# Neighbouring heads as a pair: weights in three pieces of all partitions, values in two transfers a twin, queries and keys in two halves

## The chip, the cores and the metric

The kernel runs on one core of one Trainium2 chip. The metric is the device time of one execution in microseconds; lower is better. The inputs q, k, v and the two weight matrices lie in HBM as 32-bit floats, and the output is written there as 32-bit floats.

## The reference

Cosine attention over 8 batches of 12 heads (448 tokens, 64 elements a head), then a two-layer block with a hard-swish between:

```python
q_n = q / (norm(q, axis=-1) + 1e-06)          # q, k, v: (8, 12, 448, 64)
k_n = k / (norm(k, axis=-1) + 1e-06)
scores = q_n @ k_n.T / tau                    # tau = 0.1
attn = softmax(scores) @ v
x = attn.transpose(0, 2, 1, 3).reshape(3584, 768)
h = x @ w_in                                  # (768, 2048)
out = (h * clip(h + 3, 0, 6) / 6) @ w_out     # (2048, 768)
```

## The kernel before

Two heads of a batch form a *pair*; there are 48 pairs (`HP = 6` a batch), and two successive pairs form a *twin*. The pair number n of a batch holds heads n and n + 6. The index g (0 or 1) names the head within a pair. Tokens are laid out so that partition p of 64 holds seven neighbouring tokens, and the 128 partitions hold the two pairs of a twin: partitions 0 to 63 the first pair, 64 to 127 the second.

`load_qk(j)` (line 189) loads *item* j: the queries or the keys of one twin, 448 KB. Items below 14 are queries where j is even and keys where it is odd, two items a twin. In HBM the stride from head to head is 64 times the stride from partition row to partition row, so two neighbouring heads, one of each pair of the twin, run through 128 partitions evenly, and a second dimension steps from head n to head n + 6. One DMA takes the item. `load_v(d)` (line 201) loads the values of a twin in four DMAs: for each g, and for each half of the partitions, 2 heads x 4 chunks of 64 elements. Half 0 goes to partitions 0 to 63 and half 1 to 64 to 127, with a zeroed chunk for padding.

An item then passes `square` (line 211, on ACT, GpSimd = POOL or VectorE = DVE), `reduce` (228, DVE: sums of squares), `norms` (246, four ACT steps: logarithm, exponential of half of it, logarithm with the epsilon as bias, exponential with minus one, which gives one over the norm plus epsilon), `normalise` (266), a transpose (on TensorE for items below 14, on the DMA crossbar after), and copies into `kz` and `qT` (lines 341 and following). `scores`, `exps`, `values` and `finish_values` do the attention of a pair; `vcast` (285) turns the values into 16-bit operands. The result goes transposed into `xT`, 6 chunks of 128 features, whose rows are in the order of `w_in_sb`.

`w_in_r` (line 88) is the first weight matrix as seen by the loads: features n and n + 6 heads share a chunk, so a chunk of 128 rows is two separate blocks of 64 rows, and a load of `w_in` takes 64 partitions. The list `weights` (line 902) holds eight loads, each issued by one `W` in the plan (`next_weights`, line 908, on the POOL queue, which also casts to 16 bits): four for `w_in` (each 64 partitions x 6 chunks x 1024 columns) and four for `w_out` (128 partitions). `mm1_unit(b, fc)` (line 560) multiplies column chunk fc of `w_in` with the features of batch b; it asserts how many loads must have been issued.

The order on each engine is written out by hand. `PLAN` (line 21) is a list of words for the first 18 pairs, such as `LQ.9` (load item 9), `SQ.6.a.0.7` (square item 6 on ACT), `W`, or `U` (one unit of the second part). From pair 18 on a loop (line 999) runs the same steps pair by pair. During the start TensorE runs matmuls of zeros (`DP` and `D`, lines 914 to 924) between its real work. All loads of queries, keys and values, the crossbar transposes and nearly all stores are issued from the SP queue in the plan's order. Each of these DMAs signals one of eight semaphores in turn, and an issue waits until the DMA that used its semaphore before has landed.

Of the kernel before, what the change touches and what calls it, by code (L numbers as in the profile page):

```python
# [14 lines left out]
EPS = 1e-6  # L15
# [46 lines left out]
def kernel(  # L62
# [22 lines left out]
    assert (S, D, HP, SR) == (448, 64, CC, 64)  # L85


    w_in_r = moe_w_in.tensor.rearrange("(g n p) f -> g p n f", g=2, p=64)
    w_out_r = moe_w_out.tensor.rearrange("(fc p) m -> p fc m", p=128)

    const = ctx.enter_context(tc.tile_pool(name="const", bufs=1))
# [47 lines left out]
    def raw_buffer(j):  # L139
# [3 lines left out]
    nrms = [const.tile([128, 7, 2, D], BF16, name=f"nrm{i}", tag=f"nrm{i}") for i in range(3)]  # L143
    n2s = [const.tile([128, 2, 14], FP32, name=f"n2{i}", tag=f"n2{i}") for i in range(2)]
    rs = [
        [const.tile([128, 2, 14], FP32, name=f"{x}{i}", tag=f"{x}{i}") for x in ("ln", "nr", "le", "r")]
        for i in range(2)
    ]
    bias = const.tile([128, 2], FP32, name="bias", tag="bias")
# [39 lines left out]
    def load_qk(j, *heads):  # L189
        needs(("NM", raw_before(j)))  # L190
        raw_of[j] = raw_buffer(j)
        d = j // 2
        b, n = 2 * d // HP, 2 * d % HP
        f = (q, k)[j % 2 ^ (j >= XJ)][b].rearrange("(g n) (p c) d -> n p g (c d)", g=2, c=7)[n : n + 2]
        f = f.rearrange("n p g x -> (n p) g x")
        g = slice(heads[0], heads[0] + 1) if heads else slice(0, 2)
        nc.sync.dma_start(out=raw_of[j][:, g, :, :].rearrange("p g c d -> p g (c d)"), in_=f[:, g, :])
        whole("LQ", j, heads or (0, 1))
        issued.update(("LQ", j, x) for x in heads or (0, 1))

    def load_v(d):
        needs(("VC", 2 * (d - NV)), ("VC", 2 * (d - NV) + 1))
        b, n = 2 * d // HP, 2 * d % HP
        for g in range(2):
            f = v[b, HP * g + n : HP * g + n + 2].rearrange("i (p c) d -> p i (c d)", c=7)
            t = vr[d % NV][:, 2 * g : 2 * g + 2, :, :].rearrange("p i c d -> p i (c d)")
            for half in range(2):
                o = t[64 * half : 64 * half + 64, :, (1 - half) * D : (5 - half) * D]
                nc.sync.dma_start(out=o, in_=f[:, :, 3 * half * D : (3 * half + 4) * D])

    def square(j, e, c0, n):

# [33 lines left out]
    def norms(d, *items):  # L246
        on_vector, items = "v" in items, tuple(x for x in items if x != "v")

        needs(("NM", 2 * d - 4), ("NM", 2 * d - 3))
        items = items or (0, 1)  # L250
        for x in items:
            needs(("RE", 2 * d + x))
        it = slice(items[0], items[-1] + 1)
        ln, nr, le, r = (t[:, it, :] for t in rs[d % 2])
        nc.scalar.activation(out=ln, in_=n2s[d % 2][:, it, :], func=AF.Ln)
        nc.scalar.activation(out=nr, in_=ln, func=AF.Exp, scale=0.5)
        if on_vector:
            nc.vector.tensor_scalar(out=le, in0=nr, scalar1=EPS, scalar2=None, op0=ALU.add)
            nc.vector.reciprocal(out=r, in_=le)
        else:  # L260
            nc.scalar.activation(out=le, in_=nr, func=AF.Ln, bias=eps_bias)
            nc.scalar.activation(out=r, in_=le, func=AF.Exp, scale=-1.0)  # L262
        for x in items:
            issued.add(("NO", d, x))

    def normalise(j, e, *heads):
        d = j // 2
        needs(("NO", d, j % 2), ("TR", j - 3))
        nrm = nrms[j % 3]
        nrm_of[j] = nrm  # L270
        heads = heads or (0, 1)
        g = slice(heads[0], heads[-1] + 1)
        n = len(heads)
        engines[e].tensor_tensor(  # L274
            out=nrm[:, :, g, :].rearrange("p c g d -> p g c d"),
            in0=raw_of[j][:, g, :, :],
            in1=rs[d % 2][3][:, j % 2, :]
            .rearrange("p (g c) -> p g c", g=2)[:, g, :]
            .to_broadcast([128, n, 7, D]),
            op=ALU.mult,  # L280
        )
        if whole("NM", j, heads):
            raw_of.pop(j)

    def vcast(i, e):
        needs(("LV", i // 2), ("VA", i - NVX, 3))
        t = vr[i // 2 % NV][:, i % 2, 1:5, :]
        f = bass.AP(tensor=t.tensor, offset=t.offset, ap=[t.ap[0], [9 * D, 2], [D, 4], [1, D]])
        o = vx[i % NVX][:, :, 0:D].rearrange("p (g c) d -> p g c d", g=2)
        if e == "v":  # L290
            nc.vector.tensor_reduce(out=o, in_=f.rearrange("p g c (d x) -> p g c d x", x=1), axis=AX.X, op=ALU.max)
            return
        (engines[e].copy if e == "a" else engines[e].tensor_copy)(out=o, in_=f)  # L293
# [266 lines left out]

    def mm1_unit(b, fc):
        needs(*(("CX", i) for i in range(b * HP, (b + 1) * HP)))
        assert len(weights) <= 6 - 2 * (2 * fc // FCN)
        x, g, c0 = xT[b % 2], g_of(b), b % 2 * SR
        ps, key = bank_of(None, 1)
        for cc in range(CC):
            nc.tensor.matmul(  # L567
                ps[:, 0:S],
                w_in_sb[:, cc, fc * 128 : (fc + 1) * 128],
                x[:, cc, 0:S],  # L570
                start=(cc == 0),
                stop=(cc == CC - 1),
            )
        def relu():
            u = sb.tile([128, S], BF16, name="u", tag="u", bufs=3)
            nc.scalar.activation(  # L576
                out=u[:, :], in_=ps[:, 0:S], func=AF.Relu, bias=half_bias, scale=1.0 / 6.0
            )
            post["v"].append(lambda: product(u))

        def product(u):
            nc.vector.scalar_tensor_tensor(  # L582
                out=g[:, fc, c0 : c0 + S],
                in0=u[:, :],
                scalar=1.0,
                in1=ps[:, 0:S],
                op0=ALU.min,
                op1=ALU.mult,
            )
            unread[key] = 0  # L590
            g_done.add((b, fc))

        post["a"].append(relu)
# [299 lines left out]
    for n, x in enumerate("2176"):  # L893
# [4 lines left out]
    units[NP] += [(product_unit, n, x, 2) for n, x in ((9, "7"), (9, "6"), (10, "6"))]  # L898
    units[NP] += [(product_unit, 10, "7", x) for x in range(2)]

    FG = d_ff // 2
    weights = [
        (w_in_sb[64 * g : 64 * g + 64, :, f * FG : (f + 1) * FG], w_in_r[g, :, :, f * FG : (f + 1) * FG])
        for f in range(2)
        for g in range(2)
    ] + [(w_out_sb[:, 4 * f : 4 * f + 4, :], w_out_r[:, 4 * f : 4 * f + 4, :]) for f in range(4)]

    def next_weights():
        o, w = weights.pop(0)
# [54 lines left out]


    for t in vr:
        nc.vector.memset(t[64:128, 0:2, 4, :], 0.0)
        nc.vector.memset(t[0:64, 2:4, 0, :], 0.0)
    zeros = xT[1][:, 0, :]
    nc.vector.memset(zeros, 0.0)  # L970
    nc.vector.memset(eps_bias, EPS)
    nc.vector.memset(half_bias, 0.5)
    make_identity(nc, ident)
    for t in vx:
# [123 lines left out]
```

## Time and profile before

| What | Value |
|---|---|
| Median of 3 runs | 406.0 us (405.98 to 406.21) |
| The profiled execution | 404.91 us |
| Its span | 403.1 us |
| Granted TensorE clock, mean | 1.00 |
| Busy: PE, PEld, DVE, ACT, POOL | 98%, 58%, 71%, 69%, 58% |
| Moved by DMA | 65.32 MB, mean 162 GB/s over the span |
| Loads of values from SP | 96 of 128 KB, median 4.4 us from issue to landing |
| Loads of queries and of keys from SP | 24 and 24 of 448 KB, median 4.4 and 4.9 us |
| Loads of `w_in` and of `w_out` from POOL | 4 and 4 of 768 KB, median 10.2 and 9.2 us |
| Transposes by DMA from SP | 34 into `tT`, 25 into `xT`, median 3.3 and 3.8 us |

PE is TensorE's matmuls, PEld its weight loads, SPq the sync engine's queue. The span runs from the first to the last instruction; the execution's own time is 1.8 us longer than its span, and the median of the runs 1.1 us longer than that execution. All times within the profile count from the start of the span. A size in KB of a weight load is that of the 16-bit data written; twice as much is read. A view of stretches has one row for each: its borders and length, the busy time of each engine with the number of instructions, the granted clock, the busy share of the 16 DMA engines and the GB/s that they moved. A share above 1 is possible, since packets of one engine overlap.

### The profile page before, as it was taken

Reading aid. Unit: us, or ns where it says so; the run is one execution under the profiler, and the core shown is the slowest. Engines: PE = TensorE matmul, PEld = TensorE weight load, DVE = VectorE, ACT = ScalarE, POOL = GpSimd, SP = SyncE. Lnnn points to the kernel's source line nnn. Section 1 sums busy time; section 2 is a strip of 40 time slices with the busy share of each in tenths; the row PEclk is TensorE's granted clock in tenths of the full one; section 3 lists DMA queues with packets and bytes.
Section 4 is the critical chain, followed back from the end, with each engine's and each line's share of the span. In section 5 each row is a group of like instructions: output and inputs, shape, how many; then the busy total and the mean of one; then the engine's idle time right before and its main releaser. Section 6 shows DMA issues by size and latency. Waiting matters only on the chain.

```text
span 403.1 us, 9619 instructions
## 1 busy us (share of the span) xinstructions
PE 395.5 (98%) x3696; PEld 234.3 (58%) x3696; DVE 286.4 (71%) x503; ACT 278.3 (69%) x609; POOL 234.0 (58%) x228
## 2 busy tenths in 40 slices
PE   7999999999999999999999999999999999999996
PEld 4666656555655556556555556555565556555563
DVE  5898768766998777776867888687656566644663
ACT  5999998798467686786858768668658755225230
POOL 7799655662384997488386865766665500510070
PEclk9999999999999999999999999999999999999999
DMA  8999989979988659786989659976963523130134
GB/s 289 281 254 257 216 247 230 156 125 230 187 213 220 139 128 228 171 222 130 180 216 212 152 130 164 182 192 145 192 154 76 112 46 67 41 79 21 26 73 99
DMA packets 91566, 65.32 MB, mean 162 GB/s; under 512 B 56064, under 2 KB 89984, under 8 KB 91520
## 3 DMA queue, kind: packets, MB, share of 16 engines
q1 hardware_dynamic: 87408, 58.02, 62.8%
q0 software_dynamic: 3712, 6.29, 9.0%
q8 instruction: 29, 0.48, 0.5%
q10 hardware_dynamic: 400, 0.39, 0.3%
q14 instruction: 17, 0.14, 0.1%
HBM read 47.19 MB, written 11.01 MB: 144 GB/s over the span
## 4 chain that ended last, share of the span: by engine, by line
PE 94%; DVE 3%; DMA 1%; ACT 0%; issue 0%; DVEq 0%; ACTq 0%
PE M L567 24%; PE M L740 17%; PE PV L462 13%; PE Y L567 6%; PE M L422 6%; PE Z L567 5%; PE Y L740 4%; PE Z L740 4%; PE M L614 3%; PE M L820 2%; PE Z L422 2%; PE PV L922 2%; PE Z L820 1%; PE Y L422 1%; DVE n L238 1%; PE SC L422 1%
## 5 line engine op out<-in xcount | busy, mean ns | idle before, releaser
L440 ACT ACTIVATE at<-M 128x448 bf16<-128x448 f32 x200 | 99.9, 568 | 16.4 <-PE M L422 14.4
L567 PE MATMUL M<-xT,w_in_sb 128*128 128x448 bf16 x522 | 110.8, 352 | 0.0
L567 PEld LDWEIGHTS <-w_in_sb 128*128 128x128 bf16 x768 | 72.0, 98 | 62.6 <-issue 2.8
L274 POOL TENSOR_TENSOR nrm<-big,r 128x896 bf16<-128x896 f32 (+1 forms) x48 | 79.5, 1662 | 26.1 <-ACT r L262 19.3
L576 ACT ACTIVATE u<-M,bias 128x448 bf16<-128x448 f32 x87 | 57.0, 655 | 25.2 <-PE M L567 24.8
L582 DVE SCALAR_TENSOR_TENSOR gT<-u,M 128x448 bf16<-128x448 bf16 x76 | 46.7, 618 | 36.8 <-ACT u L576 36.3
L226 POOL TENSOR_TENSOR big<-big 128x896 f32<-128x896 f32 (+3 forms) x39 | 63.9, 1641 | 10.9 <-DMA big<-in_k_dram 5.7
L462 PEld LDWEIGHTS <-at 128*128 128x128 bf16 (+1 forms) x1536 | 54.9, 97 | 22.8 <-issue 13.5
L462 PE MATMUL PV<-vx,at 128*128 128x65 bf16 (+1 forms) x1536 | 64.3, 194 | 0.2 <-DVE on L483 0.2
L238 DVE TENSOR_REDUCE n<-big 128x14 f32<-128x896 f32 (+1 forms) x50 | 51.7, 1041 | 5.6 <-ACT big L224 4.6
L379 POOL COPY km<-tT 64x128 bf16<-64x128 bf16 x34 | 12.8, 376 | 58.1 <-DMA tT<-nrm 45.1
L769 POOL TENSOR_TENSOR big<-big 128x384 f32<-128x384 f32 x11 | 11.8, 1076 | 54.6 <-ACT big L788 54.5
L740 PEld LDWEIGHTS <-gT 128*128 128x128 bf16 x288 | 27.8, 98 | 20.0 <-DVE gT L718 0.6
L740 PE MATMUL M<-w_out_sb,gT 128*128 128x384 bf16 x208 | 37.9, 326 | 0.1
L440 ACT ACTIVATE at<-Z 128x448 bf16<-128x448 f32 x49 | 27.7, 565 | 9.9 <-PE M L422 7.3
L483 DVE TENSOR_TENSOR on<-PV,rc 128x512 bf16<-128x512 f32 x48 | 33.2, 691 | 1.7
L293 POOL CAST vx<-big 128x512 bf16<-128x512 f32 x44 | 33.2, 757 | 1.2 <-DMA big<-in_v_dram 1.1
L422 PE MATMUL M<-tT,kz 64*128 64x448 bf16 (+1 forms) x175 | 31.6, 351 | 0.0
L740 PEld LDWEIGHTS <-gs 128*128 128x128 bf16 x224 | 21.5, 98 | 14.8 <-DVE gs L718 0.4
L567 PE MATMUL Y<-xT,w_in_sb 128*128 128x448 bf16 x132 | 28.6, 352 | 0.0
L440 ACT ACTIVATE at<-Y 128x448 bf16<-128x448 f32 x45 | 25.7, 570 | 3.1 <-PE Z L422 1.7
L740 PE MATMUL M<-w_sum,gs 128*128 128x384 bf16 x144 | 26.3, 326 | 0.0
(130 smaller groups left out, 561.7 us busy)
## 6 DMA issues: line engine op xcount, KB each, us to landing
big<-in_v_dram SPq DMA_DIRECT2D x96, 128.0 KB, 4.4
big<-in_k_dram SPq DMA_DIRECT2D x24, 448.0 KB, 4.9
big<-in_q_dram SPq DMA_DIRECT2D x24, 448.0 KB, 4.4
out_dram<-o SPq DMA_DIRECT2D x107, 96.0 KB, 2.2
w_in_sb<-in_moe_w_in_dram POOLq DMA_DIRECT2D x4, 768.0 KB, 10.2
w_out_sb<-in_moe_w_out_dram POOLq DMA_DIRECT2D x4, 768.0 KB, 9.2
tT<-nrm SPq DMA_TRANSPOSE x34, 3.3
xT<-on SPq DMA_TRANSPOSE x25, 3.8
```

Source lines behind the costliest of these rows:

```text
L226: engines[e].tensor_tensor(out=o, in0=i, in1=i, op=ALU.mult)
L238: nc.vector.tensor_reduce(out=n2s[d % 2][:, j % 2, c], in_=sq[:, :, :, :].rearrange("p g c d -> p (g c) d")[:, c, :], axis=AX.X, op=ALU.add,)
L274: engines[e].tensor_tensor(out=nrm[:, :, g, :].rearrange("p c g d -> p g c d"), in0=raw_of[j][:, g, :, :], in1=rs[d % 2][3][:, j % 2, :] . ...
L293: (engines[e].copy if e == "a" else engines[e].tensor_copy)(out=o, in_=f)
L422: nc.tensor.matmul(o, ks, qt[rows], start=True, stop=True)
L440: nc.scalar.activation(out=o, in_=x, func=AF.Exp, scale=inv_tau)
L462: nc.tensor.matmul(pv_out(j, h), at[rows, n, q_cols(i // HP, j)], vt[rows, 3 + h if name == "M" else 5 * h + int(name[1]), :], start=(name ...
L483: nc.vector.tensor_tensor(out=on[:, :, :, :].rearrange("p j h d -> p h j d"), in0=pv4[:, :, :, 0:D], in1=rc[:, :, :].to_broadcast([128, 2, ...
L567: nc.tensor.matmul(ps[:, 0:S], w_in_sb[:, cc, fc * 128 : (fc + 1) * 128], x[:, cc, 0:S], start=(cc == 0), stop=(cc == CC - 1),)
L576: nc.scalar.activation(out=u[:, :], in_=ps[:, 0:S], func=AF.Relu, bias=half_bias, scale=1.0 / 6.0)
L582: nc.vector.scalar_tensor_tensor(out=g[:, fc, c0 : c0 + S], in0=u[:, :], scalar=1.0, in1=ps[:, 0:S], op0=ALU.min, op1=ALU.mult,)
L740: nc.tensor.matmul(m, lhs[:, c, :], rhs[:, c, c0 : c0 + width], start=(base is None and c == 0), stop=(c == KC - 1), skip_group_check=True,)
```

## The change

A pair now holds two neighbouring heads, 2n and 2n + 1. The twin's four heads lie next to each other in HBM.

- Queries and keys: from the first pair to the second the stride is now two heads, which doesn't run on evenly from partition 63 to 64. Each item is loaded by two DMAs, one for each half of the partitions, of 64 partitions x 2 heads x 448 elements.
- Values: the four heads of a twin are one dimension, so each half of the partitions is one DMA of 64 x 4 x 256 elements. Two DMAs a twin in place of four. `vcast` and the zeroed chunks follow the new order of heads in the tile.
- `w_in`: a chunk is now 128 neighbouring rows, so a load takes all 128 partitions. Three loads of 512, 512 and 1024 columns stand in place of four, the last `W` of them leaves the plan, and the assertion in `mm1_unit` follows.
- Norms: the tile `nr` is twice as wide, with the epsilon set once in every second place, and `ln` takes the part of `le`. The ACT branch, the only one that the plan uses, keeps its four steps; two memsets are added at the start.

The order of all other instructions on TensorE, ACT, DVE and POOL stays as it was. On SP every load of an item becomes two in a row, and every four loads of values two.

```diff
-    "U RE.13 U SC.8.3 UV UA CQ.10.v VA.7.0 W RE.12 UV CQ.11.a UV UA NO.6 U EX.8.3 VA.7.1 VA.7.2 UV VC.9.p VA.7.3",
+    "U RE.13 U SC.8.3 UV UA CQ.10.v VA.7.0 RE.12 UV CQ.11.a UV UA NO.6 U EX.8.3 VA.7.1 VA.7.2 UV VC.9.p VA.7.3",
...
-    w_in_r = moe_w_in.tensor.rearrange("(g n p) f -> g p n f", g=2, p=64)
+    w_in_r = moe_w_in.tensor.rearrange("(n p) f -> p n f", p=128)
...
-        [const.tile([128, 2, 14], FP32, name=f"{x}{i}", tag=f"{x}{i}") for x in ("ln", "nr", "le", "r")]
+        [const.tile([128, 2, 14, n], FP32, name=f"{x}{i}", tag=f"{x}{i}") for x, n in (("ln", 1), ("nr", 2), ("r", 1))]
...
-        f = (q, k)[j % 2 ^ (j >= XJ)][b].rearrange("(g n) (p c) d -> n p g (c d)", g=2, c=7)[n : n + 2]
-        f = f.rearrange("n p g x -> (n p) g x")
-        g = slice(heads[0], heads[0] + 1) if heads else slice(0, 2)
-        nc.sync.dma_start(out=raw_of[j][:, g, :, :].rearrange("p g c d -> p g (c d)"), in_=f[:, g, :])
+        f = (q, k)[j % 2 ^ (j >= XJ)][b].rearrange("(n g) (p c) d -> n p g (c d)", g=2, c=7)
+        for i in range(2):
+            o = raw_of[j][64 * i : 64 * i + 64, :, :, :].rearrange("p g c d -> p g (c d)")
+            nc.sync.dma_start(out=o, in_=f[n + i])
...
-        for g in range(2):
-            f = v[b, HP * g + n : HP * g + n + 2].rearrange("i (p c) d -> p i (c d)", c=7)
-            t = vr[d % NV][:, 2 * g : 2 * g + 2, :, :].rearrange("p i c d -> p i (c d)")
-            for half in range(2):
-                o = t[64 * half : 64 * half + 64, :, (1 - half) * D : (5 - half) * D]
-                nc.sync.dma_start(out=o, in_=f[:, :, 3 * half * D : (3 * half + 4) * D])
+        f = v[b, 2 * n : 2 * n + 4].rearrange("i (p c) d -> p i (c d)", c=7)
+        t = vr[d % NV][:, :, :, :].rearrange("p i c d -> p i (c d)")
+        for half in range(2):
+            o = t[64 * half : 64 * half + 64, :, (1 - half) * D : (5 - half) * D]
+            nc.sync.dma_start(out=o, in_=f[:, :, 3 * half * D : (3 * half + 4) * D])
...
-        ln, nr, le, r = (t[:, it, :] for t in rs[d % 2])
+        ln, nr, r = (t[:, it, :, 0] for t in rs[d % 2])
...
-            nc.scalar.activation(out=le, in_=nr, func=AF.Ln, bias=eps_bias)
-            nc.scalar.activation(out=r, in_=le, func=AF.Exp, scale=-1.0)
+            nc.scalar.activation(out=ln, in_=nr, func=AF.Ln, bias=eps_bias)
+            nc.scalar.activation(out=r, in_=ln, func=AF.Exp, scale=-1.0)
...
-        t = vr[i // 2 % NV][:, i % 2, 1:5, :]
-        f = bass.AP(tensor=t.tensor, offset=t.offset, ap=[t.ap[0], [9 * D, 2], [D, 4], [1, D]])
+        t = vr[i // 2 % NV][:, 2 * (i % 2), 1:5, :]
+        f = bass.AP(tensor=t.tensor, offset=t.offset, ap=[t.ap[0], [4 * D, 2], [D, 4], [1, D]])
...
-        assert len(weights) <= 6 - 2 * (2 * fc // FCN)
+        assert len(weights) <= 6 - min(2, 4 * fc // FCN)
...
-    FG = d_ff // 2
-    weights = [
-        (w_in_sb[64 * g : 64 * g + 64, :, f * FG : (f + 1) * FG], w_in_r[g, :, :, f * FG : (f + 1) * FG])
-        for f in range(2)
-        for g in range(2)
-    ] + [(w_out_sb[:, 4 * f : 4 * f + 4, :], w_out_r[:, 4 * f : 4 * f + 4, :]) for f in range(4)]
+    pieces = [slice(f * d_ff // 4, f * d_ff // 4 + n * d_ff // 4) for f, n in ((0, 1), (1, 1), (2, 2))]
+    weights = [(w_in_sb[:, :, f], w_in_r[:, :, f]) for f in pieces] + [(w_out_sb[:, 4 * f : 4 * f + 4, :], w_out_r[:, 4 * f : 4 * f + 4, :]) for f in range(4)]
...
+    for t in rs:
+        nc.vector.memset(t[1][:, :, :, 1], EPS)
```

More of the change, by code (lines that the diff above doesn't have):

```diff
@@ L257, in norms @@
         if on_vector:
-            nc.vector.tensor_scalar(out=le, in0=nr, scalar1=EPS, scalar2=None, op0=ALU.add)
-            nc.vector.reciprocal(out=r, in_=le)
-        else:
-            nc.scalar.activation(out=le, in_=nr, func=AF.Ln, bias=eps_bias)
-            nc.scalar.activation(out=r, in_=le, func=AF.Exp, scale=-1.0)
+            nc.vector.tensor_reduce(out=ln, in_=rs[d % 2][1][:, it, :, :], axis=AX.X, op=ALU.add)
+            nc.vector.reciprocal(out=r, in_=ln)
+        else:
+            nc.scalar.activation(out=ln, in_=nr, func=AF.Ln, bias=eps_bias)
+            nc.scalar.activation(out=r, in_=ln, func=AF.Exp, scale=-1.0)
         for x in items:
@@ L276, in normalise @@
             in0=raw_of[j][:, g, :, :],
-            in1=rs[d % 2][3][:, j % 2, :]
+            in1=rs[d % 2][2][:, j % 2, :, 0]
             .rearrange("p (g c) -> p g c", g=2)[:, g, :]
@@ L966 @@
     for t in vr:
-        nc.vector.memset(t[64:128, 0:2, 4, :], 0.0)
-        nc.vector.memset(t[0:64, 2:4, 0, :], 0.0)
+        nc.vector.memset(t[64:128, 0:4:2, 4, :], 0.0)
+        nc.vector.memset(t[0:64, 1:4:2, 0, :], 0.0)
     zeros = xT[1][:, 0, :]
```

## The prediction

> **What bounds the kernel now.** I read the page first: the span, the busy shares and the slices.
>
> ```profile
> span 403.1 us, 9619 instructions
> ...
> PE 395.5 (98%) x3696; PEld 234.3 (58%) x3696; DVE 286.4 (71%) x503; ACT 278.3 (69%) x609; POOL 234.0 (58%) x228
> ...
> PE   7999999999999999999999999999999999999996
> ...
> DMA  8999989979988659786989659976963523130134
> ```
>
> TensorE is the bound: busy 98%, at full granted clock, so nothing that the change does to other engines can buy much. But the DMA slices read 8 to 9 for the first tenth and more of the span, and the stretch in which the attention pipeline fills lives on loads. There the change works. So I next asked for the waits of the start, in order of time.
>
> ```profile
> 3.80 2.71 SPq L209 DMA_DIRECT2D big<-in_v_dram  x4
> ...
> 4.31 0.67 ACT L224 ACTIVATE big<-big 128x192 f32<-128x192 f32 x2 [2.29 <-DMA big<-in_k_dram]
> ...
> 5.51 0.53 ACT L224 ACTIVATE big<-big 128x384 f32<-128x384 f32 x1 [0.54 <-DMA big<-in_q_dram]
> ...
> 7.92 4.04 SPq L209 DMA_DIRECT2D big<-in_v_dram  x4
> ...
> 16.99 1.26 DVE L291 TENSOR_REDUCE vx<-big 128x512 bf16<-128x512 f32 x2
> ```
>
> ACT starts the moment item 1 (keys) lands and again when item 0 (queries) lands. The SP queue runs far ahead of the data, so landings are set by the rate of the DMA engines, not by issuing. That rate is what the third view shows: the same engines in stretches that carry only query/key loads (rows 1, 2, 5) and only value loads (rows 3, 4, 6).
>
> ```profile
> 3.00:5.50 2.50, 2.50 (x14) 1.83 (x13) 1.37 (x9) 0.67 (x2) 1.29 (x6) 1.00 1.06 406
> 5.50:9.50 4.00, 4.00 (x22) 2.24 (x20) 2.18 (x4) 3.05 (x10) 3.18 (x4) 1.00 1.06 381
> 10.00:11.50 1.50, 1.50 (x23) 1.30 (x21) 1.50 (x2) 1.19 (x2) 0.77 (x1) 1.00 1.13 230
> 13.50:15.00 1.50, 1.50 (x15) 1.03 (x13) 1.50 (x4) 1.50 (x3) 1.50 (x2) 1.00 1.14 235
> 16.00:17.50 1.50, 1.50 (x18) 0.78 (x16) 1.50 (x4) 1.41 (x4) 0.98 (x1) 1.00 1.06 382
> 22.50:25.00 2.50, 2.35 (x34) 1.53 (x32) 2.50 (x5) 2.34 (x8) 2.48 (x3) 1.00 1.12 244
> ```
>
> The last column is GB/s. Both kinds keep the engines fully busy (share over 1), yet transfers of 128 partitions move 381 to 406 GB/s and transfers of 64 partitions 230 to 244. The packet records say the same: 1024-byte value packets take 46 ns while a 128-partition transfer is still ahead of them, then 73 to 91 ns among themselves; 1792-byte query/key packets take 74 to 79 ns, but 124 to 126 ns beside value packets. So it is not the packet size; it is that all 16 engines write one half of the partitions at a time.
>
> **Queries and keys in two halves: the price.** Today items land 1.20 us apart (4.29, 5.49, 6.70, 7.90, 9.11): 458,752 bytes at 382 GB/s. Afterwards each is two transfers of 64 partitions, alternating halves as the value loads do now. A value twin of 524,288 bytes takes 2.0 to 2.1 us (10.70 to 12.82, 14.18 to 16.19), 252 GB/s. At that rate an item takes 1.82 us: **0.62 us more per item**. Bounds: 0 if two halves in flight spread over all partitions; 0.80 if every packet takes 126 ns (16 x 126 = 2.0 us). I take 0.62, since value loads have the same shape and the same alternation.
>
> [...]
>
> Issuing: a 64-partition load costs SP 0.60 us (values), a 128-partition one 0.46. Two per item is 0.9 to 1.2 us of issue under 1.82 us of data: hidden. SP also waits for the landing of the eighth DMA before, as in the gaps at 7.92; eight halves in flight are 7 us of data, enough.
>
> **Where it reaches the path.** For each item the landing before, its first reader, the slack, and the shift (0.62 for each item up to it):
> - item 0: 5.49, ACT square 5.51, slack 0.02, shift 1.2: late **1.2**. This goes through reduce, norms and copies to the first scores (12.47).
> - item 2: slack 1.71 (7.90 to 9.61), shift 2.5: 0.8. Item 5: 1.75, shift 3.1: 1.35.
> - item 4: 10.70, POOL square 11.90, slack 1.20, shift 3.7: **2.5**. Its reduce starts on DVE 0.04 us after that square, with the copy of the next keys queued behind.
> - second value twin: 16.19, DVE cast 17.58, slack 1.40, seven items ahead, shift 4.3: **2.9**. Behind it on DVE stands the copy of the next queries (18.18), which releases scores.
> - items 7 and 8: slack 2.48 and 2.92, shift 5.0 and 5.6: 2.5 and 2.7. From 18.5 to 20.5 the engines have some 0.9 us to spare, which comes off from here.
> - item 10: 25.15, POOL square 27.23, slack 2.09, shift 6.5: POOL is 4.4 late. POOL is busy 17.8 of the 18 us from 28 to 46, so it can't catch up, but its results have 0.73 to 1.03 us before TensorE reads them (normalised item 32.90 to 33.63, cast 33.45 to 34.48). That leaves 3.4 to 3.7.
>
> TensorE follows the largest: 2.9 from the values, and up to 0.8 more from item 10. There the rate was already poor (packets of 1792 bytes at 118 to 121 ns beside the weights), so the shift is overstated: half, 0.4. **3.3 us.** After 46 us value casts and squares have 5 us and more of slack until the loop; in the loop, where TensorE is saturated, items are read 0.1 to 10 us after landing by POOL, which has idle time there (58% of the span). One transpose into xT lands 0.04 us before TensorE reads it (126.31 to 126.35), with a key load queued ahead of it on SP: 0 to 0.6; I take 0, as TensorE's 6 matmuls before it give cover when the loads shift together, and keep 0.6 for the range. A lost start is not regained by an engine that is full.
>
> **Weights.** Four loads of 64 partitions become three of 128, 768, 768 and 1536 KB; the issue at 42.89 (0.69 us of POOL) goes and the other three have more descriptors: about nothing. The first matmul that needs them starts at 42.85, 0.3 us after piece two landed; now it needs only piece one. No gain: TensorE wasn't waiting (17.73 of 18.0 us busy). Chunk 8 needs the third piece, at 58.59 + 3.3 = 61.9. Pieces three and four took 13.3 us together (40.00 to 53.33); issued 3.7 late, with three slower items beside it (1.9), it lands near 59. Cover 3 us; if that is gone, see below.
>
> **Values.** 96 transfers become 48 with the same packets to the same halves: no data time, and SP gets back 1.2 us a twin, which pays for the split items. The norms keep four ACT steps (0.21 to 0.32 us); two memsets (0.06 us each) end well before 4.31. Casts read another stride: same 0.61 us. All at nothing; if the stride mattered, 0.1 us of POOL a pair, under its idle time.
>
> **Rivals.**
> - *Not slower.* The halves overlap: engines drift apart, some write low and some high partitions, and an item keeps 1.2 us. It decides at about 0.3 us more per item: below that the second value twin is under 0.8 us late. For it: item halves are larger packets and queued eight deep. Against: the value loads, queued alike, run at 230 to 244 GB/s for microseconds. It gives 406.0, and with the lighter weight writes from 25 to 50 us at best 405.7 (TensorE idles only 0.27 us from 28 to 46). [...]
> - *The third weight piece is late.* Piece two took 13.7 us for half the bytes when loads stood beside it (28.86 to 42.55). At such a pace the big piece lands 3 us or more after chunk 8's turn, and TensorE waits: 409.3 + 3 = 412.3. Against: the SP queue runs dry at 46.55 before the loop's loads.
> - *Slack swallows most.* If only item 0's 1.2 us reaches TensorE, 407.2.
>
> **How the numbers follow.** The profiled execution took 404.9 us; plus 3.3 is 408.2. The median of the runs is 1.1 above the profiled one: 406.0 + 3.3 = 409.3. Chances: forecast 0.56, late piece 0.14, slack 0.14, not slower 0.16, of which 0.12 within 0.2% (0.8 us, about what a measurement of this kernel can tell from no change) and 0.04 faster. Range: 0.80 us per item and 0.6 in the loop give 411.2; the late piece 412.3; slack 407.2; a part of the rival of no change comes in at 406.4. So 406.4 to 412.8; slower 0.84.
>
> **What would show it.** Right: windows that carry only queries and keys at 230 to 260 GB/s; 1792-byte packets near 125 ns; item 0 near 6.7 us, the second value twin near 20.5; first scores near 13.7; first matmul of the weights near 46; from there a constant shift. Wrong: items still 1.2 us apart; DVE's second cast not behind its data; a shift that grows through the loop; TensorE waiting on weights at chunk 8.

## The result, and the profile after

The changed kernel takes 409.11 us (median of 12 runs, 408.45 to 409.94) beside 406.0 us of the kernel before (12 runs, 405.15 to 408.65): the ratio over all runs is 1.0066, with a 95% interval of 1.0048 to 1.0085, which is 2.7 us (1.9 to 3.5) of 406; the medians are 3.1 apart. The forecast was 409.3 us and slower. The profiled execution took 409.91 us against 404.91, which is 5.0 us. That overstates the change: this execution lies 0.8 us above the median of its kernel and that of before 1.1 us below. So the two profiles are used below for places and rates, and the ratios for sizes.

From the page after: the span, the busy shares, and the slices of TensorE and of the DMA engines.

```profile
span 408.0 us, 9617 instructions
...
PE 396.5 (97%) x3696; PEld 234.6 (57%) x3696; DVE 287.2 (70%) x505; ACT 278.7 (68%) x609; POOL 234.3 (57%) x227
...
PE   6798999999999999999999999999999999999996
...
DMA  8999999999999858798599849967974522231033
```

TensorE has the same 3696 matmuls and 1.0 us more of busy time, so the rest of the longer span is waiting. The slices show where: the first two and the fourth are 6, 7 and 8 in place of 7, 9 and 9, while the DMA slices read 9 without a gap from the second to the thirteenth. After that TensorE's strip is as before.

The timeline answers the lines that were shown of before (SP's issues, ACT's first squares, DVE's cast of the values). In brackets stand the idle time ahead and what ended it.

```profile
5.47 0.67 ACT L223 ACTIVATE big<-big 128x192 f32<-128x192 f32 x2 [3.45 <-DMA big<-in_k_dram]
7.41 0.52 ACT L223 ACTIVATE big<-big 128x384 f32<-128x384 f32 x1 [1.27 <-DMA big<-in_q_dram]
...
8.73 1.26 SPq L208 DMA_DIRECT2D big<-in_v_dram  x2
...
21.77 0.69 DVE L290 TENSOR_REDUCE vx<-big 128x512 bf16<-128x512 f32 x1 [0.72 <-DMA big<-in_v_dram]
```

ACT starts on the queries 1.9 us later than before (7.41 against 5.51). The second cast of values, which waited for no load in the kernel before, now does. SP issued the first value load at 8.73 us and its data landed at 16.26, so SP is still far ahead of the data.

The same stretches as before, with the granted clock, the DMA share and the GB/s in the last three columns:

```profile
3.00:5.50 2.50, 2.50 (x14) 1.83 (x13) 0.38 (x8) 0.03 (x1) 0.56 (x5) 1.00 1.06 261
5.50:9.50 4.00, 4.00 (x28) 2.45 (x25) 2.92 (x6) 2.00 (x7) 2.24 (x3) 1.00 1.08 237
10.00:11.50 1.50, 0.67 (x9) 0.51 (x9) 0.00 (x0) 1.44 (x5) 1.50 (x2) 1.00 1.09 232
13.50:15.00 1.50, 1.50 (x9) 0.43 (x6) 1.50 (x5) 1.40 (x5) 0.00 (x0) 0.50 1.10 232
16.00:17.50 1.50, 1.50 (x15) 1.03 (x13) 0.50 (x1) 1.50 (x3) 1.50 (x2) 1.00 1.11 231
22.50:25.00 2.50, 2.50 (x34) 1.47 (x34) 2.13 (x5) 2.04 (x4) 1.50 (x2) 1.00 1.08 234
```

Every stretch of the start now runs at 231 to 261 GB/s, with the engines no less busy than before (share 1.06 to 1.11). The loads of queries and keys have taken on the rate that only value loads had. The halves land 0.97 to 0.98 us apart, so an item takes 1.95 us in place of 1.20, and a packet of 1792 bytes takes 121 to 141 ns in place of 74 to 79.

The chain of work that ended last (start, length, what) says which of the late loads sets the end:

```profile
8.09 7.04 DMA big<-in_q_dram
...
15.14 8.48 DMA big<-in_k_dram
...
23.64 8.67 DMA big<-in_q_dram
...
35.00 1.69 POOL big L225
36.69 1.65 POOL nrm L273
38.39 0.56 PE Z L318 x7
```

Three loads of queries and keys follow each other, each issued when the one eight DMAs before it had landed. The last is the upper half of item 10, landed at 32.31 us. Behind it POOL squares items 10 and 11 and normalises item 7, and for that result TensorE waits with a transpose, at 38.39 us in place of 33.69. An earlier wait of the same kind belongs to item 4, whose upper half landed at 15.13: POOL squares it from 15.29 on, then normalises item 3, which TensorE transposes at 18.67 in place of 15.57. First the rows of the changed kernel, then TensorE's two of the kernel before:

```profile
16.92 1.69 POOL L273 TENSOR_TENSOR nrm<-big,r 128x896 bf16<-128x896 f32 x1
...
18.67 0.56 PE L318 MATMUL Y<-ident,nrm 128*128 128x128 bf16 x7 [0.56 <-POOL nrm L273]
...
38.39 0.56 PE L318 MATMUL Z<-ident,nrm 128*128 128x128 bf16 x7 [1.08 <-POOL nrm L273]
```

```profile
15.57 0.56 PE L319 MATMUL Y<-ident,nrm 128*128 128x128 bf16 x7
...
33.69 0.55 PE L319 MATMUL Z<-ident,nrm 128*128 128x128 bf16 x7
```

Matmul by matmul, TensorE is 1.8 us late at its first scores (14.31), 3.1 at 18.67 and 4.7 at 38.39.

### The profile page after: what moved, and what is told of

The parts are those of the page before. It is cut to its first block, busy times and chain, and to the rows that moved or that the text cites. A ratio compares the mean times of both kernels' runs of the same rounds, so it can differ in the third digit from the quotient of the medians.

```text
span 408.0 us, 9617 instructions
## 1 busy us (share of the span) xinstructions
PE 396.5 (97%) x3696; PEld 234.6 (57%) x3696; DVE 287.2 (70%) x505; ACT 278.7 (68%) x609; POOL 234.3 (57%) x227
## 4 chain that ended last, share of the span: by engine, by line
PE 87%; DMA 7%; SPq 2%; DVE 2%; POOL 1%; issue 1%; POOLq 0%
PE M L566 24%; PE M L739 16%; PE PV L461 11%; PE Y L566 6%; PE M L421 6%; PE Z L566 5%; PE Y L739 4%; DMA big<-in_q_dram 4%; PE Z L739 3%; PE M L613 3%; DMA big<-in_k_dram 2%; PE M L819 2%; SPq L197 2%; PE Z L421 1%; PE Z L819 1%; PE Y L421 1%
```

## Experiments

Each kernel was timed in turns with the kernel before on the same chip. A ratio times 406 gives the distance in us; intervals reach 0.7 to 1.3 us to each side, and the difference of two ratios is good to about 1.2 us.

### Which part costs, which part gains

**The kernel before with each item in two halves of the partitions** (`e1_parts`), and nothing else of the change:

```diff
-        nc.sync.dma_start(out=raw_of[j][:, g, :, :].rearrange("p g c d -> p g (c d)"), in_=f[:, g, :])
+        for i in range(2):
+            r = slice(64 * i, 64 * i + 64)
+            nc.sync.dma_start(out=raw_of[j][r, :, :, :].rearrange("p g c d -> p g (c d)"), in_=f[r, :, :])
```

> The kernel before, with each item of queries and keys loaded by two transfers of 64 partitions each (same bytes, same pairs of heads). If halves of the partitions are the cause: items land about 1.95 us apart in place of 1.20, GB/s in stretches of queries and keys alone near 235, the first scores near 14.3 us in place of 12.5, item 10 lands near 32, and the time is that of the changed kernel, 2.5 to 3.5 us above the kernel before. If weights or values made the loss: within 0.5 us of the kernel before.

Measured: 412.49 us, ratio 1.0155 (1.0124 to 1.0187), 6.3 us, more than twice the whole change. The start is much like that of the changed kernel; its second stretch (5.5 to 9.5 us) reads

```profile
5.50:9.50 4.00, 4.00 (x28) 2.48 (x25) 2.78 (x6) 1.79 (x7) 2.13 (x3) 1.00 1.05 240
```

But here the delay goes on growing: matmul by matmul, this profile is 4.0 us behind that of before at 33.7 us, 5.0 at 126 and 6.2 at 225. Its waits of TensorE (total, times, longest) name the place:

```profile
PE M L568 <- DMA xT<-on: 1.3, 2, 1.0
PE M L423 <- DMA tT<-nrm: 0.6, 1, 0.6
```

These are transposes by DMA, which SP issues behind the loads. With four value loads and four halves a twin, SP has eight loads where both the kernel before and the changed one have six.

**The changed kernel with whole items** (`e3_whole`). The items are again of heads n and n + 6, so queries and keys belong to other pairs than the values:

```diff
-        f = (q, k)[j % 2 ^ (j >= XJ)][b].rearrange("(n g) (p c) d -> n p g (c d)", g=2, c=7)
-        for i in range(2):
-            o = raw_of[j][64 * i : 64 * i + 64, :, :, :].rearrange("p g c d -> p g (c d)")
-            nc.sync.dma_start(out=o, in_=f[n + i])
+        f = (q, k)[j % 2 ^ (j >= XJ)][b].rearrange("(g n) (p c) d -> n p g (c d)", g=2, c=7)[n : n + 2]
+        f = f.rearrange("n p g x -> (n p) g x")
+        nc.sync.dma_start(out=raw_of[j][:, :, :, :].rearrange("p g c d -> p g (c d)"), in_=f[:, :, :])
```

> The changed kernel, with items loaded whole again, 128 partitions in one transfer of heads n and n + 6 (so that queries and keys are of other heads than the values: the output is not the reference's). If halves of the partitions are the cause of all: the time of the kernel before, within 0.8 us, TensorE not idle before the first scores, clock not lowered. If the weights in three pieces or the values in two transfers add to the loss: 0.8 us or more above the kernel before.

Measured: 404.27 us (404.06 to 405.29), ratio 0.9957 (0.994 to 0.9973): 1.7 us faster than before, which neither case of the expectation had. So the halves cost 2.7 + 1.7 = 4.4 us, and the rest of the change gives 1.7 back.

**The two other parts, each alone in the kernel before**: weights in three pieces (`e5_weights`) and values in two transfers a twin (`e6_values`). Each leaves the heads in their old pairs, so rows of the weights, or values, meet other heads than their own; only the time is of use.

```diff
-    w_in_r = moe_w_in.tensor.rearrange("(g n p) f -> g p n f", g=2, p=64)
+    w_in_r = moe_w_in.tensor.rearrange("(n p) f -> p n f", p=128)
...
+    pieces = [slice(f * d_ff // 4, f * d_ff // 4 + n * d_ff // 4) for f, n in ((0, 1), (1, 1), (2, 2))]
```

> The kernel before, with only the input weights changed: three pieces of all 128 partitions (quarter, quarter, half of the columns), one weight load of POOL less; the rows stand in the order of the changed kernel while the heads stay in the old one, so the output matrix is multiplied with rows in another order. Theory 1 (the gain that the whole-item form of the change showed, 1.75 us under the kernel before, comes from SP's shorter queue of value transfers): the weights alone are worth nothing, 405.5 to 406.5 us, and the starts of the matmuls are those of the kernel before until 126 us. [...]

```diff
-        for g in range(2):
-            f = v[b, HP * g + n : HP * g + n + 2].rearrange("i (p c) d -> p i (c d)", c=7)
-            t = vr[d % NV][:, 2 * g : 2 * g + 2, :, :].rearrange("p i c d -> p i (c d)")
-            for half in range(2):
+        f = v[b, 2 * n : 2 * n + 4].rearrange("i (p c) d -> p i (c d)", c=7)
+        t = vr[d % NV][:, :, :, :].rearrange("p i c d -> p i (c d)")
+        for half in range(2):
```

> The kernel before, with only the value loads changed: two transfers of 64 partitions x 4 heads for a twin where there were four of two heads each. The four neighbouring heads that are loaded are not those of the twin's queries and keys, so the output is that of other values. Theory 1 (SP's queue: two issues of about 0.6 us less for each of 24 twins, so that the DMA transposes behind them start earlier): 404.0 to 405.2 us, the matmuls' starts as before until about 126 us and then ever earlier, by 0.7 to 1.5 us. Theory 2 (the weights bring it): 405.7 to 406.5 us.

Measured: weights 406.33 us, ratio 1.0007 (0.9989 to 1.0025), nothing. Values 404.6 us, ratio 0.9982 (0.996 to 1.0004), 0.7 us faster with an interval that just holds no change. That is the side of theory 1, that values bring the gain, but 0.7 is short of the 1.7 of all parts together, and the expected growth of a lead in the loop was not to be read. The profiled execution was a late one (407.48 us), and it had lost its time at the start:

```profile
13.27 0.56 PE L421 MATMUL SC<-tT,kz 64*128 64x448 bf16 x4 [1.64 <-DVE tT L340]
16.09 0.37 PE L421 MATMUL SC<-tT,kz 64*128 64x448 bf16 x2 [1.31 <-ACT at L439]
```

Here item 3 landed at 8.99 us in place of 6.70, though it was issued at the same time and the engines moved 367 GB/s from 5.5 to 9.5 us. So an item that is next in line can come 2.3 us later in one execution than in another of nearly the same loads. The spread of the kernel before (404.7 to 409.4 us on one chip) may be this; no second trace shows it.

### Where in the span the halves cost

**Whole items below 14, halves after** (`e9_late_halves`) and **halves for the first four items alone** (`e11_first_four`), both from the changed kernel. The diff is that of the first; the second has `j >= 4` as its condition:

```diff
+        if j < XJ:
+            f = (q, k)[j % 2][b].rearrange("(g n) (p c) d -> n p g (c d)", g=2, c=7)[n : n + 2]
...
+            nc.sync.dma_start(out=raw_of[j][:, :, :, :].rearrange("p g c d -> p g (c d)"), in_=f[:, :, :])
+        else:
             f = (q, k)[j % 2 ^ (j >= XJ)][b].rearrange("(n g) (p c) d -> n p g (c d)", g=2, c=7)
             for i in range(2):
...
```

> The changed kernel, with the items below 14 whole (heads n and n + 6, as before) and the later ones in two halves of the partitions; the early queries and keys are so of other pairs than the values, and the output is not the reference's. It splits the cost of the halves (409.1 us of the changed kernel less 404.3 us of the one with whole items, 4.8 us) in two. Theory 1 (the cost lies in the start, where items are awaited one after another, as the prediction has it): 404.3 to 405.2 us, the matmuls as in the kernel with whole items until 60 us and at most 0.5 us later at the end. Theory 2 (much of it is the doubled number of transfers in the loop, whose issue delays the transposes behind them on SP): 405.5 to 407.0 us, with the delay growing between 126 and 280 us.

> The changed kernel with only the first four items in halves and all others whole (those of the first 14 that are whole are of heads n and n + 6, so the output is not the reference's). The first four then land as late as in the changed kernel (up to 11.23 us in place of 7.90), and the rest at the old rate. Theory 1 (a lost start is not regained, the prediction's last assumption): the matmuls stay 1.9 to 2.5 us behind the kernel with whole items to the end, 406.1 to 407.2 us. Theory 2 (what counts is the later items that end last, item 10 above all, and the early lateness is swallowed by idle filler matmuls and by buffers): 404.3 to 405.3 us.

Measured: late halves 404.86 us, ratio 0.998 (0.9961 to 0.9999); first four alone 407.12 us, ratio 1.0016 (0.9996 to 1.0035). In us from before: -0.8 and +0.6, beside -1.7 with none and +2.7 with all. So the later halves cost 0.9, the first four 2.4, and, if the three add up, the ten in between the rest of the 4.4, 1.1. The times of both runs lie where theory 1 has them. With halves for four items only, the matmuls are 2.4 us behind those of the kernel with whole items at 13 us and 2.9 to 3.1 from 16 us to the end: a start once lost is not regained, though all later items come whole. It is more than the 2.5 of theory 1, and part of it is not the loads: in that profile TensorE ran at half its clock from 13.2 to 16.6 us, eight of its filler matmuls took 1.66 us in place of 1.02, and it fell 0.6 us further back without a wait. The 0.9 of the later halves is not firm: in its profile the kernel with late halves lies 0.14 us behind the one with whole items at 225 us.

### Why two halves are slow

**Two transfers of all partitions, one for each head of the pair** (`e2_heads`), in the kernel before. Same number of transfers and of bytes as the halves:

```diff
+        for i in range(2):
+            g = slice(i, i + 1)
             nc.sync.dma_start(out=raw_of[j][:, g, :, :].rearrange("p g c d -> p g (c d)"), in_=f[:, g, :])
```

> The kernel before, with each item loaded by two transfers too, but split by head: 128 partitions of 448 elements each. As many transfers, issues and landings as with halves of the partitions. If halves of the partitions are the cause: items stay 1.20 to 1.25 us apart at 370 GB/s or more, and the time stays within 0.8 us of the kernel before. If the number of transfers (two issues of 0.5 to 0.6 us, waits for the eighth landing before) is the cause: items land 1.9 us apart and the time rises by 2.5 to 3.5 us.

Measured: 408.2 us, ratio 1.0048 (1.0029 to 1.0067), 1.9 us, where the halves cost 6.3. The rate from 5.5 us on is that of whole items:

```profile
3.00:5.50 2.50, 2.50 (x14) 1.84 (x13) 1.67 (x9) 0.67 (x2) 1.02 (x6) 1.00 0.85 242
5.50:9.50 4.00, 4.00 (x20) 2.05 (x18) 2.28 (x4) 2.00 (x8) 2.66 (x3) 1.00 1.01 367
```

In the first stretch the engines were partly idle (share 0.85), which put the start 1.0 us late; the loop then added 1.8 (1.0 us behind at 33.7, 2.8 at 272). The 1.9 us lie between the two cases of the expectation: the rate is that of the first, and the number of transfers has a price of its own: with eight loads a twin on SP, the loop loses 1.8 us here and 2.2 in the run by halves. The changed kernel has six again. Its distance to before is 4.7 us at 38.4 us and 5.1 at 131.

Where the data lies in HBM is not the cause either: a transfer by head here and a half of the changed kernel both read two neighbouring heads, 224 KB in one run, and they move 367 and 237 GB/s.

**Every other partition in place of upper and lower halves** (`e12_alternate`), in the kernel before:

```diff
+        for i in range(2):
+            o = raw_of[j][i:128:2, :, :, :].rearrange("p g c d -> p g (c d)")
+            nc.sync.dma_start(out=o, in_=f[i:128:2])
```

> The kernel before, with each item in two transfers of 64 partitions, as in the run by halves, but each transfer takes every other partition of all 128 (even ones, then odd ones) in place of the lower or the upper 64. Nothing is left out. Theory 1 (what halves the rate is where the 64 partitions lie: neighbouring ones share what leads into them): the rate in 5.5 to 9.5 us is over 330 GB/s, the packets of 1792 bytes take about 75 to 90 ns, and the time is that of the two transfers by head, 407.5 to 409 us. Theory 2 (it is the number of partitions or of rows of a transfer, wherever they lie): 230 to 260 GB/s, packets of about 125 ns, 411 to 413.5 us as in the run by halves.

Measured: 456.05 us, ratio 1.122 (1.1187 to 1.1253), far from both theories; but its first 9 us answer the question.

```profile
5.50:9.50 4.00, 4.00 (x26) 2.52 (x24) 2.21 (x5) 1.71 (x7) 1.99 (x3) 1.00 0.97 322
...
13.50:15.00 1.50, 0.00 (x0) 0.00 (x0) 1.50 (x2) 0.39 (x1) 0.00 (x0) 1.00 0.03 11
```

The median packet took 74 ns, as with whole items, and the third, fourth and fifth item each landed 1.2 to 1.7 us after the one before, at 322 GB/s, where halves of the partitions in the same kernel moved 240. Transfers of 64 partitions are thus not slow for having 64 rows: it counts which partitions they are. The rest of the run says nothing on that: from 9 us on engines wait for loads whose data they don't read. In its timeline DVE sums queries and keys only when values have landed, and SP, waiting in turn, lets the DMA engines run dry (share 0.03 in the row above).

```profile
13.49 1.08 DVE L239 TENSOR_REDUCE n<-big 128x14 f32<-128x896 f32 x1 [4.41 <-DMA big<-in_v_dram]
```

**Lower halves on SP's queue, upper halves on ACT's** (`e7_two_queues`), for the first four items of the changed kernel, issued at the very start:

```diff
-            nc.sync.dma_start(out=o, in_=f[n + i])
+            (nc.scalar if i and j < 4 else nc.sync).dma_start(out=o, in_=f[n + i])
```

> The changed kernel, with the loads of its first four items issued at the very start, the lower halves on SP's queue and the upper halves on ACT's (behind its table load, so 1.3 us later than SP's). In the changed kernel upper and lower halves take turns on one queue and move 237 GB/s from 5.5 to 9.5 us. [...] Theory 2 (the cost is in the small rows or in the number of packets, whatever the queue): 225 to 250 GB/s again, the fourth item at 10.8 to 12 us, 408.7 to 409.8 us.

Measured: 408.68 us, ratio 1.0058 (1.0034 to 1.0081), no different from the change. ACT issued its first load at 0.76 us, beside its table load (0.74 to 2.02 us) and not behind it, so upper and lower halves were in flight together from 3 to 10 us. The rate rose only a little:

```profile
5.50:9.50 4.00, 4.00 (x19) 1.95 (x17) 2.40 (x6) 1.88 (x7) 1.75 (x3) 1.00 1.07 265
```

265 GB/s in place of 237 is a little above the 225 to 250 of theory 2, and the fourth item landed at 10.69 us in place of 11.23, a little ahead of its 10.8 to 12. Having both halves in flight doesn't restore 380 GB/s: a packet took about 119 ns whether few or most of the packets beside it were of the other queue. Two queues moved 12% more than one queue on which the halves take turns.

### The clock, and two other versions

**More filler matmuls at the start of the changed kernel** (`e8_filler`), so that TensorE doesn't run idle ahead of its first transposes:

```diff
-RE.0.0 DP.8 NO.0.0 ... TR.1.Y DP.2 TR.0.Z
+RE.0.0 DP.18 NO.0.0 ... TR.1.Y DP.10 TR.0.Z
```

> The changed kernel with 18 more filler matmuls, 10 ahead of the first transposes and 8 ahead of the second, so that TensorE does not run idle at 9.5 to 10.8 and 11.6 to 12.6 us. In the profile of the changed kernel its granted clock is 0.5 from 12.3 to 15.7 us. Theory 1 (the clock is halved since TensorE ran idle, and the stretch at half clock costs nothing, since item 10's landing at 32.3 us sets the start): the granted clock is 1.0 throughout, and the time stays, 408.7 to 409.5 us. Theory 2 (the stretch costs about half its length): 407.0 to 408.2 us. Theory 3 (the clock is halved for another reason): 0.5 again.

Two of the stretches, first of the changed kernel, then with the filler (granted clock third from the end):

```profile
13.00:14.00 1.00, 1.00 (x10) 0.80 (x7) 1.00 (x3) 0.72 (x1) 0.00 (x0) 0.50 1.07 229
14.00:15.00 1.00, 1.00 (x6) 0.13 (x4) 1.00 (x3) 0.90 (x5) 0.00 (x0) 0.50 1.13 232
```

```profile
13.00:14.00 1.00, 0.82 (x12) 0.61 (x9) 1.00 (x3) 0.94 (x2) 0.00 (x0) 1.00 1.10 238
14.00:15.00 1.00, 0.78 (x7) 0.41 (x8) 1.00 (x3) 0.90 (x6) 0.02 (x1) 1.00 1.11 230
```

With the filler the clock stays at 1.0 and TensorE does the same work with idle time to spare. At 38.4 us both stand at the same place (0.2 us apart): the half clock cost nothing here, since TensorE waits for POOL's results behind it (18.67 and 38.39 us). The 12 timed runs of the changed kernel agree: three kept a mean clock of 1.0, with 408.45, 408.52 and 409.51 us, beside 408.65 to 409.94 us of the others, so the half clock costs some tenths at most. The time did not stay, though: 410.82 us (408.61 to 412.29), ratio 1.0117 (1.009 to 1.0143). Its profile loses 2.3 us in the loop, in steps at 125, 131, 187, 220 and 230 us. Why filler at 10 us should do that is open.

**A pair of every other head** (`e4_every_other`), that is, pairs (0, 2) and (1, 3) of four neighbouring heads. An item is one transfer of 128 partitions, the values two transfers a twin; the price is `w_in` in eight loads of 64 partitions x 3 chunks.

```diff
+        f = (q, k)[j % 2 ^ (j >= XJ)][b, 2 * n : 2 * n + 4].rearrange("(g n) (p c) d -> n p g (c d)", g=2, c=7)
...
+    w_in_r = moe_w_in.tensor.rearrange("(m g i p) f -> g i p m f", m=3, g=2, i=2)
```

> Another pairing: of four neighbouring heads the first pair takes the first and the third, the second pair the second and the fourth. Then the heads of the two pairs stand one behind the other in HBM and one transfer of 128 partitions takes an item, and values still go in two transfers a twin. The first weight matrix goes in eight loads of 64 partitions (every other chunk), in the four places of before. If halves of the partitions cost the time: 405.5 to 406.5, the kernel before or slightly below (SP issues 48 transfers less), first scores at 12.5 us. If neighbouring heads cost something by themselves: as slow as the changed kernel. POOL issues four more loads, some 1 us in all; its results have 0.7 us of slack there, so up to 0.5 us could come from that.

Measured: 405.34 us (404.76 to 407.94), ratio 0.9989 (0.9965 to 1.0012): level with the kernel before and 3 us better than the change. It loses 0.45 us at 33.7 us, behind POOL's additional weight loads, and has that back by 225 us. Moving its first two weight loads into an idle gap of POOL (`e13_early_weights`: the first `W` of the plan goes behind `NM.3.p`) was worse:

> The kernel of pairs of every other head (items and values in whole and in two transfers, input weights in eight loads), with its first two weight loads moved on POOL from 23.2 us to the 1.3 us in which POOL waits for ACT at 15.3 us. Nothing is left out. Theory 1 (the 0.55 us that this kernel loses at 33.7 us are POOL's two more issues ahead of the normalisation of item 10): they are won back, 404.3 to 405.2 us. Theory 2 (the loads then take bandwidth from the items and values that are awaited between 16 and 26 us): 405.5 to 408 us, with the matmuls late from 20 us on.

Measured: 409.23 us, ratio 1.0092 (1.0067 to 1.0116). The matmuls fall behind from 20.6 us on and are 6 us late at 33.7: this is the place that theory 2 names, at a higher price than the 408 us it allowed for. From 16.0 to 17.5 us, behind the moved loads, the DMA engines were busy (share 1.12) and moved 220 GB/s in all, where the kernel before moved 382. None of the versions that keep the reference's output beats the kernel before by more than the measurement can tell.

## Why the prediction was right, point by point

**The start: right in total, on another path.** The sum had 3.3 us for the halves in the start. By the ratios the first 14 items cost 3.5 (2.4 for the first four, 1.1 for the rest). The first waits (ACT on items 1 and 0) and the last (POOL's work on item 10) came where it said. The term in the middle did not: its 2.9 us were to come from the second value cast. That cast is indeed behind its data, at 21.77 us and 4.2 late, but TensorE is 3.1 late before it, at 18.67, and no later after it. The copy behind the cast had 2.1 us until its scores read it (18.55 to 20.64 in the kernel before), which the sum left out. What set the 3.1 was item 4, by way of POOL; the list had it at 2.5 and did not take it. That the term from the wrong place had nearly the right size is luck. "A lost start is not regained" was borne out by the run with four items in halves.

**The price of an item: too small.** It was set at 0.62 us more, from the value loads' 252 GB/s; it is 0.75, near the upper bound of 0.80. Items in halves run at 232 to 237 GB/s with packets of about 130 ns. Item 0 landed at 7.32 us, not 6.7, the second value twin at 21.67, not 20.5, the first scores began at 14.31, not 13.7, and the first matmul of the weights at 47.6, not 46. The upper bound was the better estimate: with every packet at 126 ns an item takes 2.0 us, and 1.95 was measured. The run with every other partition shows that it counts which 64 partitions a transfer writes: 322 GB/s against 240.

**The profile's 4.7 us at 38.4 us** are thus more than the sum's 3.3, and item 10 makes most of the difference: the sum had 0.4 for it, half of an overhang of 0.8, and it brought 1.6 (from 3.1 to 4.7). The reason given for the half, that the rate was poor there already, did not hold: the item landed 7.2 us later than before, not 6.5, and POOL squared it 5.2 us later, not 4.4. That the total still came out at 409.3 against 409.11 owes something to the base: 1.1 us were added because the profile of before lay that much under its median, but the profile of after lies 0.8 above its own.

**The loop: taken as 0, with 0.6 in the range.** The late halves cost 0.9 by the ratios and 0.1 in the profile. The place was the one named, transposes into `xT` that TensorE reads as they land:

```profile
131.49 0.35 PE L566 MATMUL M<-xT,w_in_sb 128*128 128x448 bf16 x1 [0.45 <-DMA xT<-on]
```

The kernels with late halves and with two queues have the same halves in the loop and no such wait in their profiles, so it is at the edge. What the working had as an aside, that SP's time from the value loads "pays for the split items", proved to be a term of its own: without that payment the halves cost 6.3 us, not 4.4.

**Values and weights: "all at nothing" was wrong**, by 1.7 us together. The weights alone are indeed nothing (ratio 1.0007). The values alone gave 0.7 (between a gain of 1.6 and a loss of 0.2). The step that failed is the one that freed 1.2 us of SP a twin and gave it to nobody: in the loop, transposes that TensorE awaits are queued on SP behind those loads. The traces show it at the transpose into `xT` that the kernel before reads at 126.35 us, with each kernel's own lateness at 120 us taken off:

| Loads a twin on SP | Kernels | The transpose lands at |
|---|---|---|
| 4 | whole items, every other head, early weights, values alone, first four in halves | 124.5 to 125.1 us |
| 6 | before, weights alone, late halves, two queues, the change | 125.9 to 126.7 us |
| 8 | items by head, items in halves | 126.8 and 127.3 us |

The run with more filler does not fit: it has six loads and 127.6 us, which is its loss at 131 us, and the reason is open. How much of the 1.7 comes by this way is less firm. The profile of the kernel with whole items gains 0.18 us at 126.4, 0.16 at 134.4, 0.08 at 136 and 0.30 at 225.3, 0.7 in all, and the gains at 134.4 and 225.3 are also in the profile of the run by halves, with eight loads, so they are no work of the value loads. The rest may be that the kernel before loses more in most executions than in the one profiled, which was 1.1 us under its median: the run with weights alone, which has the same loads on SP, loses 0.15, 0.40 and 0.45 us at 126, 136 and 181 us, where the kernels with whole items and with every other head lose nothing. But the run with values alone loses 0.44 at 181 too. So the way is shown and the size is not; the new layout of the norms was not run alone.

So the forecast is right in sign, in cause (items at the rate of a half, felt in the start) and in size, but the size is in part luck: two terms at zero were wrong in opposite directions (3.5 for the start, 0.9 for later halves, less 1.7, makes 2.7), and within the start one term was taken from the wrong place and one was too small.

**The rivals.** *Not slower* fell: the second stretch at 237 GB/s, an item at 1.95 us. The halves landed one after another, 0.97 us apart, and the two took 1.95 us where one of 128 took 1.20. *The third weight piece is late* fell: it landed at 59.72 us, 0.7 later than the forecast's 59, and TensorE waits for no weights. *Slack swallows most* fell with the first four items: their lateness reached the end.

## What to carry to other kernels

Price a transfer by the partitions that it writes, not only by its bytes: two loads of 64 neighbouring partitions took 1.95 us for what one load of 128 moved in 1.20, and a second queue gave little of it back (265 GB/s in place of 237, where whole items had 381). Before splitting a load to make a layout possible, look for another grouping that keeps the partitions in one run, as pairing every other head did here. And when a change frees time on a queue, look up what stands behind it there, even if the engine that issues is never the bound; a term set to zero because nobody waits for the engine may be one for which somebody waits in the queue.

## What the runs showed of the hardware that was not expected

- TensorE's granted clock fell to half from 12.3 to 15.7 us in the changed kernel, after TensorE had been busy for 54, 17 and 61% of the microseconds from 9, 10 and 11 us on. By the stretches the missing clock is 0.34 + 0.50 + 0.50 + 0.37 of a microsecond, or 3.4 us at half speed. The kernel before, with 82 and 53% from 11 and 12 us on, kept 1.0. The run by halves and the one with four items in halves show the same step, 3.41 us long each time, after 3.41 us in which TensorE was busy for 39 and 43% (41% in the changed kernel). No threshold follows: the run with early weights had such a stretch with 40% (36.2 to 39.7 us) and kept 1.0.
- Issuing a load of 64 partitions cost SP 0.61 us in the median of the changed kernel. One of 128 partitions cost 0.37 to 0.47 in the first 18 us of the kernel before, but 0.58 in the median of all its items, so the difference is mostly one of the start.
- A whole item landed 2.3 us late in one execution (8.99 us in place of 6.70), with the engines busy and the same two loads issued ahead of it.
